# Linformer attention and maxout layer: k of two more batches turned by DMA, one turn of q issued later, two waits of loads dropped

## Chip, cores and metric

The kernel runs on one core of one Trainium2 chip. The metric is device time in microseconds (us) of one execution; lower is better. Profiles come from the hardware profiler, one execution each.

## What is computed

Eight batches of eight heads, 1024 positions of width 64, float32 in and out. k and v are first projected from 1024 positions to 64 by two shared matrices, then comes ordinary attention on the 64 projected positions, then a layer that takes the maximum of three products.

```python
k_proj = einsum('ks,bhsd->bhkd', E, k)        # 64 x 64 per head
v_proj = einsum('ks,bhsd->bhkd', F, v)
scores = matmul(q, k_proj.T) / sqrt(64)       # 1024 x 64 per head
attn   = softmax(scores)
y      = matmul(attn, v_proj)                 # 1024 x 64 per head
x      = y.transpose(0, 2, 1, 3).reshape(8192, 512)
h      = maximum(maximum(x @ w1, x @ w2), x @ w3)   # 8192 x 768
out    = h @ w_out                            # 8192 x 512
```

## The kernel before

**Stages.** The loop over batches (line 869) runs the maxout layer of batch b, and between its steps it places the attention of batch b+1. A batch has two chunks (`ch` 0 and 1) of 512 positions. A chunk is six steps of `up` (line 717; 12 matmuls each, three weight matrices by four row blocks, then a copy on ScalarE at line 733 and two maxima on VectorE at lines 737 and 678), and four steps of `down` (line 767; six matmuls each, a copy on ScalarE, and a store of 512 KB after every second one, line 792). So a chunk has steps 0 to 9, and (1, 3) in what follows is step 3 of chunk 1.

**Attention of a batch.** `load` (line 198) brings q, k and v in by three DMAs that GpSimd issues; they turn float32 into bfloat16 on the way. `qd` (line 411) lays out q in the tile `q_p` by four copies on VectorE, and then SyncE issues one DMA that transposes the whole of it, 128 x 4096, into `qT` (line 424). `kproj` (line 496) projects k: 16 matmuls and a copy to the tile `kp`, 128 x 256. Then `kp` has to be turned into `kpT`. There are two ways: `kt` (line 504) does it with two transposes on TensorE into a bank of the accumulation memory and a copy on VectorE; `kd` (line 521) does it with one DMA transpose that SyncE issues (line 524). `sc` (line 331) computes scores of a pair of heads from `qT` and `kpT` (line 221) and their exponential (line 232). `zc` (line 258) sums exponentials, inverts the sums on ScalarE, writes them to a scratch in memory (`zd`, line 278) and reads them back over all partitions with four broadcast DMAs of 512 KB (line 285). `vproj` (line 529) projects v; `vx` (line 293) multiplies the exponentials by it (line 241) and by the inverted sums (line 318), into `xT`, the input of the next batch's layer.

**Order of the work.** Each engine executes its instructions in the order in which the program writes them; the framework adds the semaphore waits for data. `plan` (line 809) is the list, written by hand, of what goes behind which step. TensorE's order is therefore `up` and `down` of batch b with the pieces of batch b+1 in between, and SyncE's queue has the stores, the scratch write and the broadcasts of `zc`, the turns of q and the turns of k, in program order. SyncE waits at the head of its queue; what comes later waits behind it. Banks of the accumulation memory are dealt out by a small model of the clock (`two`, `bank`, line 77), to whoever is free first.

For batch 2's layer, which carries the attention of batch 3 and the start of batch 4, the plan is

```python
(0, 2): [kproj(3), vproj(3), ld(4)],
(0, 3): [kt(3)],
(0, 4): [sc(3, 0, now=True), sc(3, 1)],
(0, 5): [sc(3, 2, now=True), sc(3, 3, now=True)],
(0, 7): [zc(3)],
(0, 8): [qd(4)],
(1, 3): [kproj(4), vproj(4), ld(5), vx(3, 0), vx(3, 1)],
(1, 4): [kt(4)],
(1, 7): [vx(3, 2), vx(3, 3), sc(4, 0)],
```

Batches 5, 6 and 7 already use `kd`. They are placed by the general branch at line 853 (there n = b + 1), in the layers of batches 3, 4 and 5: there kproj(n + 1), kd(n + 1) and vproj(n + 1) stand at (1, 2), and sc(n + 1, 0) four steps later, at (1, 6); the turn of q of that batch is issued at (0, 4).

**Waits added by hand.** In `load`, the DMA of q waits for the last turn of q before it (`last_T`, line 202) and, where that batch's k was turned by DMA, for that turn too (`turned`, line 204). k and v follow it in GpSimd's queue. `k_pair` (line 207) picks the layout of `kpT`: the two ways leave the pairs of heads in different places.

Of the kernel before, what the change touches and what calls it, by code (L numbers as in the profile page):

```python
# [15 lines left out]
def kernel(  # L16
# [13 lines left out]
    nc = tc.nc  # L30
# [9 lines left out]
    SI = 8  # L40
    NCT = DM // P
    NJT = DF // P
    NPAIR = H // 2
# [38 lines left out]
    def bank():  # L82
        n = min(range(8), key=lambda n: free[n])
        deal((n,))
        return psum_t[:, n, :], (n,)
# [15 lines left out]
    def copy(eng, o, i, ns=(), dt=0.65):  # L101
        done = {  # L102
            "v": nc.vector.tensor_copy, "s": nc.scalar.copy, "g": nc.gpsimd.tensor_copy
        }[eng](out=o, in_=i)
        runs(eng, clock["pe"] if ns else 0.0, dt, ns)
        return done

    def after(dma, earlier):
        tc.add_manual_dep(
            dma.ins, earlier.ins.name,  # L110
            mybir.DependencyInfo(
                mybir.DependencyClass.Sync, mybir.DependencyReason.DATA
            ),
        )


    def view(src, b):
        return src[b].rearrange("h (p si) d -> p h si d", si=SI)
# [12 lines left out]
    qkv, qTs, kpTs, vps, pTs, zis, xTs = {}, {}, {}, {}, {}, {}, {}  # L131
    last_T = {}
# [4 lines left out]
    def load_tiles(b):  # L137
        qkv[b] = tuple(
            loads.tile([P, H, SI, D], BF16, name=nm, bufs=n)
            for nm, n in (("q_t", 2), ("k_t", 1), ("v_t", 1))  # L140
        )
        return qkv[b]
# [55 lines left out]
    def load(b, which):  # L198
        tiles = qkv[b] if b in qkv else load_tiles(b)
        for i in which:  # L200
            dma = nc.gpsimd.dma_start(out=tiles[i], in_=view((q, k, v)[i], b))  # L201
            if i == 0 and b - 1 in last_T:
                after(dma, last_T[b - 1])
            if i == 0 and b - 1 in turned:
                after(dma, turned[b - 1])

    def k_pair(b, g):
        if b in turned:
# [3 lines left out]
    turned = {}  # L212
# [80 lines left out]
    def vx(b, g):  # L293
        def f():
            scale_x(b, g, 0, SI, values(b, g, 0, SI))
        return f
# [13 lines left out]
    def values(b, g, lo, nsi):  # L310
        if b not in xTs:
            xTs[b] = att.tile([P, NCT, SI, P], BF16, name="xT")
        return pair_mm(b, g, lo, nsi, lambda rows, hp: vps[b][rows, 2 * g + hp, :])

    def scale_x(b, g, lo, nsi, av):
        t, ns, ready = av
        zi, when = zis.pop((b, g, lo))
        nc.vector.tensor_tensor(  # L318
            out=xTs[b][:, g, lo:lo + nsi, :].rearrange("a (c s) p -> a c (s p)", c=2),
            in0=t, in1=zi, op=ALU.mult,  # L320
        )
        runs("v", max(ready, when), 0.17 + nsi * 0.13, ns)
# [28 lines left out]
    def proj(b, kv, t, heads, width):  # L351

        for si in range(SI):
            for hh in range(2):
                nc.tensor.matmul(  # L355
                    out=t[hh * HALF:(hh + 1) * HALF, 0:width],
                    lhsT=efT[:, si, (kv - 1) * KP:kv * KP],
                    rhs=qkv[b][kv][:, heads[hh], si, :],
                    start=(si == 0), stop=(si == SI - 1),
                )  # L360
        pe(8 * (width * 0.00042 + 0.01))
# [46 lines left out]

    q_ps = {}

    def qd(b, gs=range(NPAIR), eng="v"):

        def f():
            lo, n = gs[0], len(gs)
            if lo == 0:
                q_ps[b] = att.tile([P, NPAIR, SI, 2, D], BF16, name="q_p", bufs=1)
                qTs[b] = att.tile([P, NPAIR * SI, P], BF16, name="qT")
            q_p = q_ps[b]
            for g in gs:
                copy(  # L420
                    eng, q_p[:, g].rearrange("p si h d -> p h si d"),
                    qkv[b][0][:, 2 * g:2 * g + 2], (), 0.43,
                )
            last_T[b] = nc.sync.dma_start_transpose(
                out=qTs[b][:, lo * SI:(lo + n) * SI, :],
                in_=q_p[:, lo:lo + n].rearrange("p g si h d -> p (g si h d)"),
            )
        return f

    class Duo:  # L430
# [65 lines left out]
    def kproj(b):  # L496
        def f():
            t, ns = bank()
            proj(b, 1, t, (LO, HI), 4 * D)
            kps[b] = att.tile([P, 2, 2 * D], BF16, name="kp")  # L500
            copy("v", kps[b].rearrange("a g x -> a (g x)"), t[:, 0:4 * D], ns, 0.43)
        return f

    def kt(b):
        def f():
            t, ns = two()
            t = t.bitcast(BF16)[:, 0]
            for gg in range(2):
                nc.tensor.transpose(
                    out=t[:, gg * P:(gg + 1) * P], in_=kps[b][:, gg, :], identity=ident  # L510
                )
            pe(0.2)

            kpTs[b] = att.tile([P, NPAIR, KP], BF16, name="kpT")
            copy(
                "v", kpTs[b].rearrange("a (y x) k -> a x y k", x=2),
                t[:, 0:2 * P].rearrange("a (x y k) -> a x y k", x=2, y=2), ns, 0.3,
            )
        return f

    def kd(b):
        def f():
            kpTs[b] = att.tile([P, 2, 2 * KP], BF16, name="kpT2")
            turned[b] = nc.sync.dma_start_transpose(
                out=kpTs[b], in_=kps[b].rearrange("a g x -> a (g x)")
            )
        return f

    def vproj(b):
        def f():  # L530
            t, ns = bank()
            proj(b, 2, t, (LO, HI), 4 * D)

            vps[b] = att.tile([P, H, D], BF16, name="vp")
            for hh, hs in enumerate((LO, HI)):
                i = t[hh * HALF:(hh + 1) * HALF, 0:4 * D].rearrange("a (h d) -> a h d", d=D)
                for to in range(2):
                    copy("sv"[hh], vps[b][to * HALF:(to + 1) * HALF, hs, :], i, ns, 0.4)
        return f
# [266 lines left out]
    def ld(b, which=(0, 1, 2)):  # L806
        return lambda: load(b, which)

    def plan(b):
        n = b + 1  # L810
        if b == 0:
            return {
                (0, 6): [
                    duo[1].sums, duo[1].values, duo[0].scale, duo[1].invert,
                ],
                (0, 7): [
                    qd(1, range(2)), duo[1].scale, qd(1, range(2, 4), "s"), store_now,
                ],
                (1, 1): [kproj(1)],
                (1, 2): [kt(1)],  # L820
                (1, 3): [sc(1, 0, now=True), sc(1, 1), vproj(1), ld(2)],
                (1, 4): [za(1, 0), sc(1, 2, now=True)],
                (1, 5): [za(1, 1), sc(1, 3)],
                (1, 7): [za(1, 2)],
                (1, 8): [za(1, 3)],
            }
        if b == 1:
            return {
                (0, 0): [qd(2)],
                (0, 3): [kproj(2), vproj(2), ld(3, (0,))],  # L830
                (0, 4): [kt(2)],
                (0, 5): [sc(2, 0, now=True), sc(2, 1, now=True), sc(2, 2)],
                (0, 6): [sc(2, 3, now=True)],
                (0, 8): [zc(2, nc.gpsimd), ld(3, (1, 2))],
                (1, 1): [qd(3)],
                (1, 3): [vx(2, 0), vx(2, 1)],
                (1, 6): [vx(2, 2), vx(2, 3)],
            }
        if b == 2:
            return {  # L840
                (0, 2): [kproj(3), vproj(3), ld(4)],
                (0, 3): [kt(3)],
                (0, 4): [sc(3, 0, now=True), sc(3, 1)],
                (0, 5): [sc(3, 2, now=True), sc(3, 3, now=True)],
                (0, 7): [zc(3)],
                (0, 8): [qd(4)],
                (1, 3): [kproj(4), vproj(4), ld(5), vx(3, 0), vx(3, 1)],
                (1, 4): [kt(4)],
                (1, 7): [vx(3, 2), vx(3, 3), sc(4, 0)],
            }  # L850
        if n == B:
            return {}
        out = {
            (0, 1): [sc(n, 1, now=True), sc(n, 2, now=True), sc(n, 3)],
            (0, 3): [zc(n)],
            (1, 2): [vx(n, 0), vx(n, 1)],
            (1, 6): [vx(n, 2), vx(n, 3)],
        }
        if n + 1 < B:
            out[0, 4] = [qd(n + 1)]  # L860
            out[1, 2] = [kproj(n + 1), kd(n + 1), vproj(n + 1)] + out[1, 2]
            out[1, 6] += [sc(n + 1, 0)]
        if n + 2 < B:
            out[1, 3] = [ld(n + 2)]
        return out

    duo = [Duo(u, SPC) for u in range(2)]

    for b in range(B):
        p = plan(b)  # L870

        def behind(ch, step):
# [61 lines left out]
```

## Time and profile before

| what | value |
|---|---|
| runs of the kernel | 399.17, 399.23, 399.59 us (median 399.23) |
| the profiled execution, its own time | 399.43 us |
| its span, first to last instruction | 397.7 us |
| TensorE busy with matmuls (PE) | 390.7 us, 98% |
| VectorE (DVE) busy | 201.9 us, 51% |
| ScalarE (ACT) busy | 152.3 us, 38% |
| GpSimd (POOL) busy | 34.5 us, 9% |
| DMA row q0 (issued by GpSimd) | 29104 packets, 30.41 MB |
| DMA row q1 (issued by SyncE) | 38064 packets, 35.46 MB |
| granted TensorE clock | 0.999 |

Of the 399.43 us, 1.7 lie before the first and after the last instruction. PE is the matmul part of TensorE, PEld its weight loads; SPq is SyncE's queue as it issues DMAs. A busy time is the sum of the records of an engine. Matmul records overlap one another (a 512-column matmul has a record of 379 ns, and the next starts 216 ns after it), so a gap on TensorE is read from the distance of two starts and not from the busy time. The chain that ended last is followed back from the last instruction to what released each step. The trace also has a record of each DMA packet, with start, duration, size and row.

### The profile page before, as it was taken

The page shows a single profiled execution, that of the slowest core. Times are in us where ns is not written, and L with a number is a line of the kernel's source. Part 1 is how long each engine was busy: PE and PEld are TensorE (multiplying, and loading weights), DVE is VectorE, ACT ScalarE, POOL GpSimd, SP SyncE. Part 2 cuts the span into 40 slices and gives each one's busy share as a digit, 9 for nine tenths or more (in the row PEclk, how much of TensorE's full clock was granted, in tenths as well). Part 3 has the DMA queues.
Part 4 walks back from the last instruction along what each step waited for, and adds up shares of the span by engine and source line. Part 5 has one row for each costly group of instructions (what it writes and reads, how often), then busy time and mean ns, then how long its engine had stood idle before and what let it go on. Part 6 is the DMA issues. An engine that isn't in the chain of part 4 may idle for free.

```text
span 397.7 us, 5745 instructions
## 1 busy us (share of the span) xinstructions
PE 390.7 (98%) x2286; PEld 176.7 (44%) x2286; DVE 201.9 (51%) x312; ACT 152.3 (38%) x239; POOL 34.5 (9%) x49
## 2 busy tenths in 40 slices
PE   7999999999999999999999999999999999999996
PEld 3544443453445445444454445444454444444443
DVE  2348756761764535645374544745266443745251
ACT  2435638527222552253323532245323533132322
POOL 7350011000400200200002000200000000000000
PEclk9999999999999999999999999999999999999999
DMA  8999999987999999999979979696970138020203
GB/s 147 206 206 207 205 248 142 244 155 159 235 181 263 147 228 206 220 176 207 215 208 147 246 174 276 91 236 115 222 208 39 69 86 237 0 105 2 105 0 107
DMA packets 67339, 66.31 MB, mean 167 GB/s; under 512 B 31504, under 2 KB 59792, under 8 KB 67312
## 3 DMA queue, kind: packets, MB, share of 16 engines
q0 software_dynamic: 29104, 30.41, 47.6%
q1 hardware_dynamic: 38064, 35.46, 34.8%
q8 instruction: 18, 0.29, 0.3%
q14 instruction: 9, 0.07, 0.1%
q10 hardware_dynamic: 144, 0.07, 0.1%
HBM read 69.73 MB, written 16.97 MB: 218 GB/s over the span
## 4 chain that ended last, share of the span: by engine, by line
PE 93%; DVE 2%; DMA 2%; ACT 1%; issue 1%; POOL 0%; DVEq 0%; ACTq 0%; POOLq 0%
PE banks L668 61%; PE banks L776 20%; PE banks L355 3%; PE banks L241 2%; DMA k_t<-in_k_dram 2%; PE banks L221 2%; DVE xT L318 1%; PE banks L266 1%; ACT zi_all L307 1%; ACT zl L301 1%; PE banks L575 1%; DVE m L737 0%; PE banks L546 0%; PE banks L601 0%; PE banks L756 0%
## 5 line engine op out<-in xcount | busy, mean ns | idle before, releaser
L668 PE MATMUL banks<-xT,w_sb 128*128 128x512 bf16 x1152 | 257.1, 379 | 0.3 <-DVE xT L318 0.3
L668 PEld LDWEIGHTS <-w_sb 128*128 128x128 bf16 x1152 | 110.2, 98 | 136.6 <-issue 8.4
L737 DVE TENSOR_TENSOR m<-banks,h1s 128x512 f32<-128x512 f32 x90 | 62.1, 690 | 134.0 <-ACT h1s L733 90.1
L733 ACT COPY h1s<-banks 128x512 f32<-128x512 f32 x90 | 52.7, 585 | 122.1 <-PE banks L668 120.6
L776 PE MATMUL banks<-wout_sb,hT 128*128 128x512 bf16 x378 | 86.6, 380 | 0.1
L678 DVE TENSOR_TENSOR hT<-banks,m 128x512 bf16<-128x512 f32 x90 | 62.3, 692 | 9.4
L776 PEld LDWEIGHTS <-hT 128*128 128x128 bf16 x378 | 35.4, 98 | 47.7 <-issue 5.7
L102 ACT COPY o_sb<-banks 128x512 f32<-128x512 f32 (+2 forms) x57 | 32.9, 578 | 57.8 <-PE banks L776 57.3
L318 DVE TENSOR_TENSOR xT<-banks,zi_all 128x1024 bf16<-128x1024 f32 x28 | 33.1, 1220 | 11.7 <-PE banks L241 6.9
L232 ACT ACTIVATE pT<-banks 128x1024 bf16<-128x1024 f32 (+1 forms) x32 | 30.2, 974 | 15.4 <-PE banks L221 15.4
L201 POOL DMA_DIRECT2D q_t<-in_q_dram x7 | 6.2, 880 | 196.8 <-DMA qT<-q_p 85.1
L355 PEld LDWEIGHTS <-efT 128*64 128x64 bf16 x224 | 11.6, 110 | 3.4 <-issue 3.4
L102 DVE CAST vp<-banks 64x256 bf16<-64x256 f32 (+1 forms) x18 | 7.1, 397 | 11.7 <-ACT vp L102 9.0
L102 ACT CAST vp<-banks 64x256 bf16<-64x256 f32 x14 | 5.1, 365 | 18.3 <-PE banks L355 18.3
L241 PE MATMUL banks<-pT,vp 64*64 64x512 bf16 (+1 forms) x128 | 10.3, 375 | 0.2 <-DVE vp L102 0.2
L221 PE MATMUL banks<-qT,kpT 64*64 64x512 bf16 (+1 forms) x128 | 9.7, 372 | 0.4 <-DVE m L737 0.4
L102 DVE COPY q_p<-q_t 128x1024 bf16<-128x1024 bf16 x26 | 9.7, 433 | 0.5 <-DMA q_t<-in_q_dram 0.5
L102 DVE COPY o_sb<-banks 128x512 f32<-128x512 f32 (+1 forms) x9 | 5.6, 640 | 5.4 <-PE banks L756 4.5
L546 PE MATMUL banks<-warm_f 128*128 128x512 f32 x8 | 6.6, 977 | 1.5 <-DVE warm_f L175 1.5
L301 ACT ACTIVATE zl<-banks 128x512 f32<-128x512 f32 (+1 forms) x8 | 6.5, 811 | 3.3 <-PE banks L241 3.1
L355 PE MATMUL banks<-k_t,efT 128*64 128x256 bf16 x112 | 7.4, 276 | 0.0
L355 PE MATMUL banks<-v_t,efT 128*64 128x256 bf16 x112 | 7.3, 273 | 0.0
(73 smaller groups left out, 125.4 us busy)
## 6 DMA issues: line engine op xcount, KB each, us to landing
out_dram<-o_sb SPq DMA_DIRECT2D x30, 512.0 KB, 4.5
zi_all<-zd SPq DMA_DIRECT2D x20, 512.0 KB, 7.8
q_t<-in_q_dram POOLq DMA_DIRECT2D x7, 1024.0 KB, 10.4
k_t<-in_k_dram POOLq DMA_DIRECT2D x7, 1024.0 KB, 17.3
v_t<-in_v_dram POOLq DMA_DIRECT2D x7, 1024.0 KB, 21.9
zi_all<-zd POOLq DMA_DIRECT2D x4, 512.0 KB, 7.4
w_sb<-in_moe_w_dram POOLq DMA_DIRECT2D x4, 384.0 KB, 10.9
k_t<-in_k_dram POOLq DMA_DIRECT2D x2, 512.0 KB, 9.2
```

The source lines that it names most:

```text
L102: done = {"v": nc.vector.tensor_copy, "s": nc.scalar.copy, "g": nc.gpsimd.tensor_copy}[eng](out=o, in_=i)
L221: nc.tensor.matmul(out=t[c * HALF:(c + 1) * HALF, hp, 0:n * P], lhsT=k_pair(b, g)[rows], rhs=qTs[b][rows, at:at + n, :], start=True, stop= ...
L232: nc.scalar.activation(out=pTs[b, g, lo], in_=t, func=AF.Exp, scale=scale)
L241: nc.tensor.matmul(out=t[hp * HALF:(hp + 1) * HALF, c, 0:nsi * HALF], lhsT=w(rows, hp), rhs=p[rows, hp, :], start=True, stop=True,)
L301: nc.scalar.activation(out=zl, in_=t, func=AF.Ln)
L318: nc.vector.tensor_tensor(out=xTs[b][:, g, lo:lo + nsi, :].rearrange("a (c s) p -> a c (s p)", c=2), in0=t, in1=zi, op=ALU.mult,)
L355: nc.tensor.matmul(out=t[hh * HALF:(hh + 1) * HALF, 0:width], lhsT=efT[:, si, (kv - 1) * KP:kv * KP], rhs=qkv[b][kv][:, heads[hh], si, :], ...
L668: nc.tensor.matmul(out=h, lhsT=w_sb[i][:, ct, jt * P:(jt + 1) * P], rhs=xTs[b][:, ct, ch * SPC:(ch + 1) * SPC, :], start=(ct == first), st ...
L678: nc.vector.tensor_tensor(out=o, in0=h, in1=other, op=ALU.max)
L733: nc.scalar.copy(out=h1s, in_=h[0][0])
L737: nc.vector.tensor_tensor(out=m12, in0=h[1][0], in1=h1s, op=ALU.max)
L776: nc.tensor.matmul(out=o_ps, lhsT=hTs[b, ch][:, jt, tt * P:(tt + 1) * P], rhs=wout_sb[:, jt, :], start=(jt == 0), stop=(jt == NJT - 1),)
```

## The change

Batches 3 and 4 use `kd` in place of `kt`, directly behind their `kproj`. `qd` gets a switch, so that its copies stay at (0, 8) and the DMA of batch 4's turn of q is issued at (1, 2) by a new `qd_turn`. In SyncE's queue this puts one instruction, the store behind step (0, 9), ahead of that turn; the broadcasts of batch 3 were ahead of it already. The hand-made wait of loads for the turn of k is taken out of `load`, for all batches; the wait for the turn of q stays.

```diff
@@ load
             if i == 0 and b - 1 in last_T:
                 after(dma, last_T[b - 1])
-            if i == 0 and b - 1 in turned:
-                after(dma, turned[b - 1])
@@ qd
+    def qd_turn(b, gs=range(NPAIR)):
+        def f():
+            lo, n = gs[0], len(gs)
+            last_T[b] = nc.sync.dma_start_transpose(
+                out=qTs[b][:, lo * SI:(lo + n) * SI, :],
+                in_=q_ps[b][:, lo:lo + n].rearrange("p g si h d -> p (g si h d)"),
+            )
+        return f
+
-    def qd(b, gs=range(NPAIR), eng="v"):
+    def qd(b, gs=range(NPAIR), eng="v", turn=True):
...
-            last_T[b] = nc.sync.dma_start_transpose(
-                out=qTs[b][:, lo * SI:(lo + n) * SI, :],
-                in_=q_p[:, lo:lo + n].rearrange("p g si h d -> p (g si h d)"),
-            )
+            if turn:
+                qd_turn(b, gs)()
@@ plan, b == 2
-                (0, 2): [kproj(3), vproj(3), ld(4)],
-                (0, 3): [kt(3)],
+                (0, 2): [kproj(3), kd(3), vproj(3), ld(4)],
                 (0, 4): [sc(3, 0, now=True), sc(3, 1)],
                 (0, 5): [sc(3, 2, now=True), sc(3, 3, now=True)],
                 (0, 7): [zc(3)],
-                (0, 8): [qd(4)],
-                (1, 3): [kproj(4), vproj(4), ld(5), vx(3, 0), vx(3, 1)],
-                (1, 4): [kt(4)],
+                (0, 8): [qd(4, turn=False)],
+                (1, 2): [qd_turn(4)],
+                (1, 3): [kproj(4), kd(4), vproj(4), ld(5), vx(3, 0), vx(3, 1)],
                 (1, 7): [vx(3, 2), vx(3, 3), sc(4, 0)],
```

## Prediction

> **What bounds the kernel now.** I read the page's busy shares first, then the shares of the chain, then the chain and the timelines of TensorE and SyncE around batch 4's start, then the answers on the turned tiles.
>
> ```profile
> PE 390.7 (98%) x2286; PEld 176.7 (44%) x2286; DVE 201.9 (51%) x312; ACT 152.3 (38%) x239; POOL 34.5 (9%) x49
> PE 93%; DVE 2%; DMA 2%; ACT 1%; issue 1%; POOL 0%; DVEq 0%; ACTq 0%; POOLq 0%
> ```
>
> TensorE sets the end. A change pays only by taking matmuls from TensorE or closing a gap in its starts, and costs only by opening one. After 75 us the start records show hardly a gap besides the two around 164 us, where the change works. The chain there (start, length, what):
>
> ```profile
> 162.10 0.28 DVE kpT L102
> 162.39 0.61 DVE m L737
> 163.09 0.70 DVE hT L678
> 163.84 1.68 PE banks L776 x7
> 166.08 0.39 PE banks L221 x4
> ```
>
> TensorE waits for VectorE's last maximum, which was held up by the copy of kpT. Then its weight loads, just ahead of the scores of batch 4:
>
> ```profile
> 165.69 0.11 PEld L221 LDWEIGHTS <-kpT 64*64 64x64 bf16 x1
> 166.05 0.11 PEld L221 LDWEIGHTS <-kpT 64*64 64x64 bf16 x3 [0.25 <-issue]
> ```
>
> kpT was there at 165.69, but qT was not: the scores started at 166.05. What SyncE did before:
>
> ```profile
> 143.14 0.49 SPq L278 DMA_DIRECT2D zd<-zic  x1
> 148.49 2.60 SPq L285 DMA_DIRECT2D zi_all<-zd  x4
> 151.20 12.83 SPq L424 DMA_TRANSPOSE qT<-q_p  x1
> 164.13 6.12 SPq L792 DMA_DIRECT2D out_dram<-o_sb  x3
> qT<-q_p SPq DMA_TRANSPOSE x1, 14.8
> ```
>
> The turn of q occupies SyncE's queue from 151.20 to 164.03, because its packets stand behind 2 MB of broadcasts, and lands at 151.20 + 14.8 = 166.0. So the scores of batch 4 already start just when their input lands. The turns of k that the kernel has (batches 5 to 7; first line ns in the queue, second us to landing):
>
> ```profile
> L524 SPq DMA_TRANSPOSE kpT<-kp x3: 1181/1185/2200, 202.3 to 293.5; - x3
> DMA to landing us min/median/max: 3.0/4.1/5.0
> ```
>
> **What the Trainium skill says.** "DMA: Bandwidth & Descriptors", section "Queues, rings and completion order": on each DMA engine the descriptors of one row are consumed in ring order, and an engine goes round robin between rows by packets. The trace agrees: batch 4's turn of q has no bulk of packets before the broadcasts' last one (159.3), and batch 3's turn, beside loads of the other row, ran at 152 packets/us against 1132 alone. Hence k's turn, issued behind q's in the same row, can't overtake it. "TensorE: Matmul & The Clock Gate", section "Part 4: PE-mode transpose", gives about 275 ns for a transpose in a kernel and a copy after it; here the record is 219 ns, the distance to the next start 56 ns, the copy 0.28 us. I use the trace's.
>
> **The change, part by part.**
>
> *TensorE loses two transposes in batch 3 and two in batch 4.* Starts in batch 4: transposes at 159.82, next matmul at 159.93; batch 3: 131.89 and 132.00. So 0.11 us each, all on the path: −0.22.
>
> *VectorE loses two copies of 0.28.* Batch 3's, at 132.70, is followed by a maximum after 1.02 idle: nothing. Batch 4's is on the chain shown. Without it hT lands at 163.51 and TensorE can go on at 163.56; it gets there, 0.11 earlier than now, at 163.49 (five starts 216 ns apart, the fifth at 163.38, less 0.11). The gap of 163.38 to 163.84, 0.24 over the usual distance, shrinks to 0.07. So this point comes 163.84 − 163.56 = 0.28 earlier, the batch's own transposes included; with batch 3's 0.11, if VectorE's start follows, 0.39. TensorE would be ready for the scores at 165.70 + 0.22 − 0.39 = 165.53 in place of 166.05: **0.52 us is all that the removals can give**, and only if qT and kpT are there.
>
> *k's turn of batch 3 on SyncE.* kp is ready at 128.95 (cast 128.53 + 0.42), and SyncE has been free since 126.4. Landing: at least 3.0 after issue, so 132.0. Its packets (records: 256 of 256 B) stand behind two stores, whose last packets run at 129.5. The existing turns landed 2.1 to 2.6 after the packets ahead of them: 202.29 + 5.0 = 207.3 against 205.1; 247.10 + 4.1 = 251.2 against 248.6; 293.50 + 3.0 = 296.5 against 294.4. That gives 132.1 at most alone. Batch 4's loads start at 128.79, their packets from 130: at 152 per us the 256 take 1.7 us instead of 0.2, hence 133.6. The scores of batch 3 need it at 134.68 − 0.11 = 134.57. I take nothing: the matmuls of steps (0, 3) and (0, 4) hide it by 1.0. Its cost is between nothing and, if the tail of the landing is stretched too (135.5, an estimate), 1.0. The loads of batch 4 are held back by under 1.7 us; the scratch's landing, for which the broadcasts wait, may move by as much, because the loads end at 150 and the broadcasts' packets start as they end.
>
> *One store ahead of q's turn.* Batch 2's store of step (0, 9), now at 164.13, is issued at 151.1. It is 128 packets of 4 KB; their records after 165.5 run for 1.15 us. Placed between broadcasts and turn it puts the turn's packets back by that, or by nothing if the turn's descriptors were what was late.
>
> *q's turn.* Its bulk of 4096 packets ended 6.25 us after the last broadcast (159.3 to 165.55) in batch 4; in batches 5 to 7 it was 4.75, 4.15 and 4.3 (198.1 to 202.85, 242.1 to 246.25, 287.6 to 291.9). Batch 4's has two near-empty stretches, at 160 and 162. With the broadcasts ending at 159.2 the new end is 159.2 + 1.15 + (4.15 to 6.25) = 164.5 to 166.6. I take 165.6: the middle, and where it is now.
>
> *k's turn of batch 4.* kp is ready at 156.3, but SyncE is in q's turn until 1.5 us before that turn's end (164.03 against 165.55), 164.1. It is issued then: 164.1 + 3.0 = 167.1 at least; by packets ahead plus 2.1 to 2.6, with 165.6, 167.7 to 168.2. With both ends of q's turn: 166.6 to 169.2. I take 167.8. Until now kpT was ready at 162.38 and the turn of q was late; now the turn of k behind it is next late, by more. Behind the waiting scores on TensorE are batch 2's last two `down` steps and batch 3's layer, so nothing covers it. Scores start 0.05 after landing (166.0 to 166.05 today), at 167.85: **+1.8 us**, net of all removals, because they end in this wait. The ends are +0.6 and +3.2.
>
> *Waits of loads.* Batch 4's and 5's loads keep the wait for q's turn. Batch 5's moves with it, within 1 us; its k landed at 184.7 and is used at 199.2: nothing. Batches 6 and 7 lose the wait for k's turn and start up to 3 us earlier (208.22, 251.74 now). Their k's turn would then share with the load: 207.3 + 1.5 = 208.8 at worst, needed at 211.35. Nothing; without that cover it would cost 1.5 each.
>
> *Banks.* `kt` no longer takes two banks, so the dealing rotates for what follows. No view prices that: −0.3 to +0.3, taken at 0, since steady batches show no gap to win.
>
> Sum: profiled execution 399.43 + 1.8 = 401.2. That execution is 0.2 above the median of the runs (399.23), so I predict **401.0**.
>
> **Rivals.**
>
> *Everything lands in time.* With the store hidden in the stretches in which q's turn starved, q's bulk may end at 164.0 or before, and k's tail be shorter, 1.5. For: those empty stretches, and batches 5 to 7 with 4.2. Against: the tail was never under 2.1. It decides where k lands before 165.5; then −0.5 us, 398.7, not slower. Between this and the forecast lies a landing up to 166.8.
>
> *k of batch 3 is late as well.* Loads of batch 4 start at the same moment. If it lands at 135.5, TensorE waits 1.0 at (0, 4), and with +1.8 the time is 402.0; with the late end of k's turn of batch 4, 403.4. For: the packets of batch 3's q, seven times slower beside loads. Against: 256 packets only.
>
> *The change does only its dealing.* If k's turn of batch 4 were issued ahead of q's, or banks decided, the time would be 399.2 ± 0.3. SyncE's program order speaks against it.
>
> **How the numbers follow.** Forecast 0.70 (400.0 to 402.5). In time or nearly 0.16 (398.7 to 400.0). k of batch 3 late 0.10 (401.5 to 403.4). Dealing alone or something unseen 0.04 (398.4 to 400). A measurement here can tell about 0.2%, 0.8 us: under 398.4 is faster, over 400.0 slower. No part can give 0.8, so faster gets 0.03, from the unseen; same 0.17; slower 0.80. The range is 399.6 to 402.6: it leaves out the early third of "in time", faster, and the worst of batch 3's lateness.
>
> **What would show it.** In the new trace: SyncE's k turn directly behind q's near 164, landing near 167.8, and a gap of some 2 us in TensorE's starts ahead of L221 there, with the weight load itself waiting now. No gap at batch 3's scores near 134.5. The hT gap at 163.8 gone. Distances between batches from 170 on unchanged. Wrong if k of batch 4 lands before 166, if the gap is at batch 3's scores, or if gaps appear in later batches.

## The result, and the profile after

The changed kernel takes 401.38 us (median of 6 runs, 400.89 to 402.79) against 399.56 us for the kernel before (6 runs, 399.17 to 399.83): +1.82 us, ratio 1.0053 with a 95% interval of 1.0035 to 1.0072. (Ratios here are taken over all runs, so they are not the quotients of the medians.) I had predicted 401.0. The sum came out; the terms did not, as the profile shows at once. The profiled execution is the one of 402.79 us, the longest of the six, so its waits are larger than the median's.

The page of the changed kernel, busy times and shares of the chain (the lines shown of before were 98% and PE 93%, DMA 2%):

```profile
PE 386.8 (96%) x2240; PEld 176.1 (44%) x2282; DVE 201.5 (50%) x310; ACT 152.2 (38%) x239; POOL 34.4 (9%) x49
PE 91%; DMA 5%; ACT 1%; issue 1%; DVE 1%; POOL 0%; SPq 0%; DVEq 0%; ACTq 0%; POOLq 0%
```

There are four weight loads fewer (2286 to 2282: the four transposes) and two VectorE instructions fewer (312 to 310: the copies). The matmul records are 42 short of the weight loads, so some are missing from the trace and PE's 386.8 is not to be compared; DMA's share of the chain, from 2 to 5%, is. The chain between 126 and 172 us names both places (start, length, what):

```profile
128.45 0.43 DVE kp L102
128.89 0.02 issue
128.90 8.51 DMA kpT<-kp
137.42 0.04 issue
137.46 0.63 PE banks L219 x8
...
167.18 2.31 DMA kpT<-kp
169.48 0.04 issue
169.53 0.41 PE banks L219 x4
```

The turn of k of batch 3, issued at 128.90, took 8.51 us to land, and TensorE waited for it at batch 3's scores. The turn of k of batch 4 took 2.31 us and ended the second wait. SyncE's queue at these points:

```profile
128.90 1.18 SPq L529 DMA_TRANSPOSE kpT<-kp  x1
...
151.00 2.61 SPq L283 DMA_DIRECT2D zi_all<-zd  x4
153.71 0.64 SPq L797 DMA_DIRECT2D out_dram<-o_sb  x1
154.46 12.63 SPq L412 DMA_TRANSPOSE qT<-q_p  x1
167.18 1.20 SPq L529 DMA_TRANSPOSE kpT<-kp  x1
```

The order is the one that the prediction used: broadcasts, one store, q's turn for 12.63 us, and k's turn directly behind it. In the kernel before, batch 3's scores had started at 134.68 without a wait for kpT; an idle time of 0.42 ahead of these weight loads is usual:

```profile
134.68 0.14 PEld L221 LDWEIGHTS <-kpT 64*64 64x64 bf16 x8 [0.42 <-DVE m L737]
```

Starts of the same instructions in the two profiles tell where time is lost:

| first instruction of | before | after | later by |
|---|---|---|---|
| scores of batch 3 | 134.68 | 137.46 | 2.78 |
| projection of k of batch 4 | 154.79 | 157.57 | 2.78 |
| vx(3, 2), just ahead of batch 4's scores | 165.45 | 168.03 | 2.58 |
| scores of batch 4 | 166.05 | 169.53 | 3.48 |
| next scores of batch 4 | 174.27 | 177.74 | 3.47 |
| last instruction (span) | 397.7 | 401.0 | 3.3 |

2.78 of it arises at batch 3's scores, where the prediction had put nothing. 0.20 comes back between the next two rows, where the removed transposes and the copy ahead of hT were. 0.90 arises at batch 4's scores. After that the two traces run in step.

### The profile page after: what moved, and what is told of

The parts are those of the page before. It is cut to its first block, busy times and chain, and to the rows that moved or that the text cites. A ratio compares the mean times of both kernels' runs of the same rounds, so it can differ in the third digit from the quotient of the medians.

```text
span 401.0 us, 5698 instructions
## 1 busy us (share of the span) xinstructions
PE 386.8 (96%) x2240; PEld 176.1 (44%) x2282; DVE 201.5 (50%) x310; ACT 152.2 (38%) x239; POOL 34.4 (9%) x49
## 4 chain that ended last, share of the span: by engine, by line
PE 91%; DMA 5%; ACT 1%; issue 1%; DVE 1%; POOL 0%; SPq 0%; DVEq 0%; ACTq 0%; POOLq 0%
PE banks L673 60%; PE banks L781 20%; PE banks L353 3%; DMA kpT<-kp 3%; PE banks L239 2%; DMA k_t<-in_k_dram 2%; PE banks L219 2%; PE banks L264 1%; DVE xT L316 1%; ACT zi_all L305 1%; ACT zl L299 1%; PE banks L580 1%; PE banks L551 0%; PE banks L606 0%; PE banks L761 0%
## 5 line engine op out<-in xcount | busy, mean ns | idle before, releaser
L673 PE MATMUL banks<-xT,w_sb 128*128 128x512 bf16 x1119 | 254.1, 379 | 2.4 <-issue 0.6
L781 PE MATMUL banks<-wout_sb,hT 128*128 128x512 bf16 x370 | 85.5, 379 | 0.9 <-issue 0.6
L219 PEld LDWEIGHTS <-kpT 64*64 64x64 bf16 x128 | 2.9, 105 | 10.0 <-DMA kpT<-kp 4.7
```

The lines of the kernel that those rows point to most:

```text
L219: nc.tensor.matmul(out=t[c * HALF:(c + 1) * HALF, hp, 0:n * P], lhsT=k_pair(b, g)[rows], rhs=qTs[b][rows, at:at + n, :], start=True, stop= ...
L673: nc.tensor.matmul(out=h, lhsT=w_sb[i][:, ct, jt * P:(jt + 1) * P], rhs=xTs[b][:, ct, ch * SPC:(ch + 1) * SPC, :], start=(ct == first), st ...
L781: nc.tensor.matmul(out=o_ps, lhsT=hTs[b, ch][:, jt, tt * P:(tt + 1) * P], rhs=wout_sb[:, jt, :], start=(jt == 0), stop=(jt == NJT - 1),)
```

## The experiments

Three theories. A: batch 3's k is late because batch 4's loads start beside it, and batch 4's because store, turn of q and turn of k all have to pass SyncE's row ahead of the scores. B: the turn of batch 3's k is slow behind the two stores ahead of it in its row, and the loads do not matter. C, my prediction: only batch 4 counts. All times are against runs of the kernel before that were taken beside them on the same chip. Loads don't wait for k's turn in any of these kernels, as in the changed one, except where a run says so.

### Batch 3 alone

```diff
@@ from the changed kernel, plan, b == 2
-                (0, 8): [qd(4, turn=False)],
-                (1, 2): [qd_turn(4)],
-                (1, 3): [kproj(4), kd(4), vproj(4), ld(5), vx(3, 0), vx(3, 1)],
+                (0, 8): [qd(4)],
+                (1, 3): [kproj(4), vproj(4), ld(5), vx(3, 0), vx(3, 1)],
+                (1, 4): [kt(4)],
```

> Only batch 3's k is turned by DMA; batch 4 keeps TensorE's transposes and its old turn of q; the loads don't wait for k's turn. Theory A (batch 4's loads, which start at the same moment, stretch k's turn of batch 3): it lands 5 us or more after its issue, TensorE waits 1 to 3 us at batch 3's scores, the time is 1 to 2.8 us over before. Theory B (the turn of k is slow behind the two stores in its own row, whatever the loads do): the same here. Theory C (my prediction: only batch 4's turn counts, and batch 3's wait in the profile was one execution's accident): no wait at batch 3's scores, -0.1 us.

Measured: 400.60 against 399.41 us, +1.19; ratio 1.0042 (1.0014 to 1.0070). The runs spread from 399.22 to 404.67. In the profiled execution the turn took 6.4 us from issue to landing, and the weight load at batch 3's scores waited:

```profile
kpT<-kp SPq DMA_TRANSPOSE x1, 6.4
135.46 0.14 PEld L219 LDWEIGHTS <-kpT 64*64 64x64 bf16 x8 [1.27 <-DMA kpT<-kp]
```

1.27 idle where 0.42 is usual: 0.85 lost in this execution. Theory C falls: batch 3's lateness is no accident of one execution, but its size varies, from about nothing to several microseconds. Not all of the spread is landing: the two longest runs, 403.01 and 404.67 us, also have the lowest mean clocks of the nine, 0.995 and 0.996 against 0.998 to 1.000.

### Batch 4 alone

```diff
@@ from the changed kernel, plan, b == 2
-                (0, 2): [kproj(3), kd(3), vproj(3), ld(4)],
+                (0, 2): [kproj(3), vproj(3), ld(4)],
+                (0, 3): [kt(3)],
```

> Batch 3 keeps TensorE's transposes; batch 4's k is turned by DMA behind the late turn of q. Theories A and B: TensorE waits about 1 us at batch 4's scores, 0.5 to 1.2 us over before. Theory C: the whole +1.8 us is here.

Measured: 400.58 us, +1.17; ratio 1.0024 (1.0012 to 1.0035), and hardly any spread (400.33 to 400.78). As A expected. SyncE's queue:

```profile
151.62 0.67 SPq L797 DMA_DIRECT2D out_dram<-o_sb  x1
152.40 12.40 SPq L412 DMA_TRANSPOSE qT<-q_p  x1
164.90 1.20 SPq L529 DMA_TRANSPOSE kpT<-kp  x1
```

q's turn landed at 152.40 + 14.4 = 166.8 and k's at 164.90 + 2.3 = 167.2. So k's turn ended only 0.4 after q's, and scores started at 167.24. The two single runs add up to 2.36; the whole change costs 1.82. The spread of batch 3's part is larger than that difference, so I draw nothing from it.

### The load waits for k's turn again

```diff
@@ from the changed kernel, load
             if i == 0 and b - 1 in last_T:
                 after(dma, last_T[b - 1])
+            if i == 0 and b - 1 in turned:
+                after(dma, turned[b - 1])
```

> The changed kernel with the removed lines put back: the load of q waits for k's turn too. Theory A: k's turn of batch 3 lands about 3 us after its issue and the wait at batch 3's scores is gone; batch 4's loads start some 4 us later and end as much later, the broadcasts of batch 3 with them, so that the turns of batch 4 may come 1 to 4 us later than in before: +1 to +4 us in all, the wait now at batch 4's scores. Theory B: the wait at batch 3's scores stays. Theory C: no wait at batch 3's scores here nor without the lines; +1.8 us in both.

Measured: 402.88 us, +3.47; ratio 1.0080 (1.0066 to 1.0094). GpSimd's queue issued batch 4's loads at 131.76 in place of 128.05, and k's turn, in the same place of SyncE's queue behind the same stores, now took 2.3 us:

```profile
125.28 1.00 SPq L799 DMA_DIRECT2D out_dram<-o_sb  x2
128.88 1.17 SPq L531 DMA_TRANSPOSE kpT<-kp  x1
kpT<-kp SPq DMA_TRANSPOSE x1, 2.3
```

It landed at 131.2, 3 us ahead of the scores, and there was no wait there. Everything else being as in the changed kernel, 8.5 became 2.3 us when the loads stood back. That speaks for A and against B. But the cost moved and grew. q's turn of batch 4 landed at 168.0 (152.80 + 15.2; 166.8 in the run of batch 4 alone), k's at 168.4, and the weight load at batch 4's scores waited:

```profile
168.44 0.11 PEld L221 LDWEIGHTS <-kpT 64*64 64x64 bf16 x4 [2.98 <-DMA kpT<-kp]
...
169.14 0.15 PEld L783 LDWEIGHTS <-hT 128*128 128x128 bf16 x1 [0.25 <-issue]
169.57 0.15 PEld L783 LDWEIGHTS <-hT 128*128 128x128 bf16 x1 [0.28 <-issue]
```

Behind the wait the weight loads take 0.15 in place of 0.10 us and follow one another in 0.43 in place of 0.22. The stretches before, in and after it show why; the columns are the stretch, its length, busy time of PE, PEld, DVE, ACT and POOL, the granted clock, the DMA share and GB/s:

```profile
160.00:168.40 8.40, 5.69 (x31) 2.12 (x29) 5.79 (x7) 1.75 (x3) 0.00 (x0) 1.00 1.07 225
168.40:173.00 4.60, 4.34 (x15) 1.73 (x17) 0.00 (x0) 1.48 (x2) 2.63 (x3) 0.63 0.77 167
173.00:178.00 5.00, 5.00 (x25) 2.25 (x23) 1.73 (x3) 1.79 (x4) 0.00 (x0) 1.00 1.13 158
```

For 4.6 us the clock was 0.63: at that rate 4.6 x 0.37 = 1.7 us are lost, on top of a wait of 2.5. Three of the six runs show this loss in their mean clock (0.994 to 0.995, 402.90 to 403.50 us), three don't (0.999 to 1.000, 401.88 to 402.87 us). So leaving this hand-made wait out was not the fault; with it the median is worse by 1.65, and the median of the three runs without the loss, 401.92, is still 2.5 over the kernel before.

### k's turn in the middle of the loads

```diff
@@ from the changed kernel
+    def k_behind_q_load():
+        after(turned[3], q_loads[4])
...
-                (0, 2): [kproj(3), kd(3), vproj(3), ld(4)],
+                (0, 2): [kproj(3), vproj(3), ld(4), kd(3), k_behind_q_load],
```

> The changed kernel with k's turn of batch 3 made to wait until batch 4's q has landed, so that it runs in the middle of the loads of k and v and not at their start. TensorE waits for it at batch 3's scores in any case, some 8 us; what counts is the time from its issue to its landing. If any load beside it stretches it: 5 us or more, as in the profiles with the load starting beside it (6.4 and 8.5). If only a load's start does it: 2.3 to 3.5 us.

Measured: 411.6 us, nearly all of it the 10 us for which TensorE waits by construction and the slow clock behind that. `q_loads` holds the DMA of q that `load` issues. What counts is SyncE's issue and the time to landing:

```profile
137.33 1.18 SPq L535 DMA_TRANSPOSE kpT<-kp  x1
kpT<-kp SPq DMA_TRANSPOSE x1, 6.7
```

6.7 us in the steady middle of the loads of k and v, with no store ahead in its row. So it is not only the start of a load that stretches a turn. Packet records show two shapes of it. Where the load's packets were already running, the turn's came late: in the changed kernel's profile the load's ran from 129.6 and k's 256 packets from 133.5 to 136.9, the first 4.6 us after SyncE's issue; here the first came at 141.2, 3.9 us after it. In the run of batch 3 alone k's packets came first, through by 130.9, and the load's from 130.65; there the 4-byte packets of SyncE's row, which I take to report completion, came only at 134.0 to 135.2. With the loads held back they came at 130.5 to 130.9. Why a few hundred packets wait that long is not settled by these runs.

### The store alone

```diff
@@ from the kernel before, with qd and qd_turn of the changed one, plan, b == 2
-                (0, 8): [qd(4)],
+                (0, 8): [qd(4, turn=False)],
+                (1, 2): [qd_turn(4)],
```

> The kernel before with one thing changed: batch 4's turn of q is issued at (1, 2), so behind one store. By the prediction's term the turn lands 0 to 1.15 us later, which the scores of batch 4 feel in full: 0 to +1.1 us. If the turn's own descriptors are what is late, 0.

The loads' wait for k's turn stands here as in the kernel before. Measured: 400.24 against 399.41 us, +0.83; ratio 1.0022 (1.0014 to 1.0030, 22 runs). q landed at 152.81 + 14.2 = 167.0 and the scores started at 167.05, 0.87 after the weight load ahead of them (0.36 in the kernel before). The term of the prediction, 0 to 1.15 and fully felt, holds.

### Batch 4's k ahead of its q

```diff
@@ from the run of batch 4 alone, plan, b == 2
-                (1, 2): [qd_turn(4)],
-                (1, 3): [kproj(4), kd(4), vproj(4), ld(5), vx(3, 0), vx(3, 1)],
+                (1, 3): [kproj(4), kd(4), qd_turn(4), vproj(4), ld(5), vx(3, 0), vx(3, 1)],
```

> Batch 3's k by TensorE; batch 4's k turned by DMA ahead of its turn of q in SyncE's queue, and the store of step (0, 9) ahead of both. If the order of k behind q costs, k lands long before batch 4's scores and they wait for q alone; q lands as in the run with only the store moved. Theory A: between +0.5 and +0.9 us over before, some 0.4 under the run with k behind q (+1.17). If k's place doesn't matter: +1.2 us again.

Measured: 400.31 against 399.45 us, +0.86; ratio 1.0021 (1.0012 to 1.0030). As with the store alone, and TensorE's wait now is for qT. k's place behind q is worth the difference to +1.17, some 0.3 us, but across these two runs that is within the noise. Against the run of the store alone, taken beside that of batch 4 alone, it is 0.34 (95% interval, resampled from the runs: 0.04 to 0.57), barely clear of it.

### Batch 4's turn of q where it was

```diff
@@ from the run of batch 4 alone, plan, b == 2
-                (0, 8): [qd(4, turn=False)],
-                (1, 2): [qd_turn(4)],
+                (0, 8): [qd(4)],
```

> Batch 3's k by TensorE, batch 4's turn of q where it was in before (ahead of the store), batch 4's k turned by DMA behind it. Theory A (the store is most of batch 4's cost, k's turn ends 0.4 us after q's): k lands near 166.4, +0.3 to +0.5 us. The prediction's working (k lands 2.1 to 2.6 us after q's last packet): near 167.7, +1.7 us.

Measured: 400.70 us, +1.25; ratio 1.0037 (1.0022 to 1.0052). My expectation missed, because I forgot where the store then stands:

```profile
151.18 12.45 SPq L412 DMA_TRANSPOSE qT<-q_p  x1
163.73 0.53 SPq L797 DMA_DIRECT2D out_dram<-o_sb  x1
164.36 1.39 SPq L529 DMA_TRANSPOSE kpT<-kp  x1
```

q lands early again, at 151.18 + 14.4 = 165.6, but the store now lies between the two turns, and k lands at 164.36 + 2.9 = 167.3. So between the two turns the store costs what it costs ahead of both (+1.17), within the noise: in both places store, q and k all have to pass before the scores. Moving q's turn behind the store, as the change does, cost nothing that shows beside this alternative. The store behind q and k in that order was not tried.

### The store behind both turns

```diff
@@ from the run with k ahead of q
-            if (b, ch, tt) == (0, 0, 1):
+            if (b, ch, tt) in ((0, 0, 1), (2, 0, 3)):
                 stores.append(store)
...
-                (1, 3): [kproj(4), kd(4), qd_turn(4), vproj(4), ld(5), vx(3, 0), vx(3, 1)],
+                (1, 3): [kproj(4), kd(4), qd_turn(4), store_now, vproj(4), ld(5), vx(3, 0), vx(3, 1)],
```

> As the run with k ahead of q for batch 4 (+0.85), but the store of step (0, 9) is issued behind both turns. If the store is what remained of batch 4's cost, q lands about 1 us earlier, near 165.3 to 166.0, and the time is -0.5 to 0 us against before. If it is q's turn itself that is late once it waits for batch 4's kp (issued near 157 and not at 151): +0.5 us or more, as with the store ahead.

A store in `stores` is kept back until `store_now` issues it.

Measured: 399.26 against 399.34 us; ratio 1.0001 (0.9993 to 1.0009). Batch 4's cost is gone. SyncE's queue shows the price of it:

```profile
148.79 2.60 SPq L283 DMA_DIRECT2D zi_all<-zd  x4
156.37 1.20 SPq L529 DMA_TRANSPOSE kpT<-kp  x1
157.66 5.96 SPq L412 DMA_TRANSPOSE qT<-q_p  x1
163.71 6.18 SPq L797 DMA_DIRECT2D out_dram<-o_sb  x3
```

q's turn is issued 6 us later than in the kernel before (157.66 against 151.20) and lands no later: 157.66 + 8.0 = 165.7. It had only been waiting in SyncE's queue behind the broadcasts' packets; 5.96 us of issue replace 12.83.

### Batch 3's k one step earlier

```diff
@@ from the run of batch 3 alone, plan, b == 2
-                (0, 2): [kproj(3), kd(3), vproj(3), ld(4)],
+                (0, 1): [kproj(3), kd(3)],
+                (0, 2): [vproj(3), ld(4)],
```

> Only batch 3's k by DMA, as in the first run of this kind (+1.2), but its projection and turn one step earlier, at (0, 1): issued near 126.4, 2 us ahead of the loads. Theory A (loads beside it stretch it): it lands before 131, no wait at batch 3's scores, -0.3 to +0.2 us. Theory B (it is slow behind the two stores of its row): issued while both are in the row, it still lands 5 us or more after issue; its scores may hide that, so the time from issue to landing decides.

Measured: 399.30 against 399.34 us; ratio 0.9996 (0.9987 to 1.0004), 398.75 to 399.73 in 13 runs. Both the cost and the spread of batch 3's turn are gone. Issued at 126.52, behind both stores, it landed 4.3 us later, at 130.8:

```profile
kpT<-kp SPq DMA_TRANSPOSE x1, 4.3
```

Most of that was ahead of the load, whose packets ran from 129.6. Theory B's 5 us or more didn't come.

### The waits of loads alone

```diff
@@ from the kernel before, load
-            if i == 0 and b - 1 in turned:
-                after(dma, turned[b - 1])
```

> The kernel before without the loads' wait for k's turn, which batches 6 and 7 have; nothing else changed. Prediction's term and theory A: k's turns of batches 5 and 6 are four steps ahead of their scores, so 0 (within 0.3 us). Rival: the earlier loads stretch those turns as they do batch 3's, and the scores of batch 5 or 6 wait: +1 us or more.

Measured: 399.35 against 399.45 us; ratio 0.9994 (0.9985 to 1.0003). No time is lost, as predicted, but the turn of batch 6 was stretched all the same. The three turns of k here, which were 3.0, 4.1 and 5.0 us in the kernel before:

```profile
DMA to landing us min/median/max: 3.7/5.1/8.0
```

The 8.0 is batch 6's. In the kernel before this turn took 4.1 us and the next load waited for it; here the load starts at 246.32, 0.7 us ahead of the turn. The turn lands at 255.0 and is used at 257.3, so the distance hides it. Batch 6 is a control that every run has: in the ten profiles of kernels without the wait its turn took 6.6 to 8.3 us, in the three with it (before, the store alone, the load waiting again) 4.0 to 4.4. Without the wait the load's packets start 0.9 to 1.5 us after the turn's issue, and the turn's own end 5.7 to 7.8 us after it, against 3.1 to 3.8 with the wait. Batch 7's, with no load beside it, took 2.8 to 3.7 in all thirteen. So theory A's reading of the load doesn't rest on batch 3 alone.

### Both remedies

```diff
@@ from the run with the store behind both turns, plan, b == 2
-                (0, 2): [kproj(3), vproj(3), ld(4)],
-                (0, 3): [kt(3)],
+                (0, 1): [kproj(3), kd(3)],
+                (0, 2): [vproj(3), ld(4)],
```

> Both remedies: batch 3's k one step earlier, batch 4's k and q turns ahead of the store. If both causes are right nothing waits for a turn of k: -0.6 to 0 us against before, the best of all. If the wait at either batch's scores stays: +0.5 us or more.

Measured: 399.10 against 399.34 us; ratio 0.9993 (0.9984 to 1.0002). No wait for a turn of k is left. It has the lowest median of all the kernels, but the interval includes 1: a kernel faster than before is not shown, and the removals' bound of 0.5 us says why not much can be.

## Why the prediction was right, and where it wasn't

**What bounds.** That TensorE sets the end, that the removals can give no more than 0.52 us, and that the change must pay in waits for turned tiles, held. With every such wait taken away the gain was 0.24 us, within the measurement of nothing.

**k's turn of batch 3: the step that failed.** I took nothing: a landing at 133.6, 4.6 us after issue, hidden by 1.0 us, with a cost of at most 1.0. It costs about 1.2 on the median of its own run, 0.85 and 2.78 in two profiles. I had reckoned the load as a lower packet rate only (1.5 us more) and named the stretched tail as a mere bound. Landing took 6.4, 8.5 and 6.7 us beside loads, and 2.3 without. The term for the waits of batches 6 and 7 has the same fault: it allowed 1.5 us of stretch, and batch 6's turn took 3.9 more; only its distance saved it. The trace of before had a sign of such a delay. Batch 3's turn of q was issued at 105.35 with nothing ahead of it in its row, and its first packet came at 110.98, just as the last of the broadcasts in GpSimd's row ended (111.01). I took this turn's rate beside the loads and not its late start. The Trainium skill's page "DMA: Bandwidth & Descriptors", section "Issuing engines are not separate DMA queues", says that DMAs from all queues run on the same engines and interleave. Once begun, k's packets did run among the load's (133.5 to 136.9 in the changed kernel's profile); of the late start and the late completion the section says nothing.

**k's turn of batch 4: the wait right, its terms mis-sized.** I had +1.8 there, all of it on k's place: q's last packet was to stay at 165.6, store included, and k to land 2.1 to 2.6 us after it. By itself batch 4's part costs 1.17. In that profile q's last packet came near 166.3, so 0.7 later, and k landed at 167.2, 0.9 after it and 0.4 after q. The 2.1 to 2.6 came from turns behind stores. Of the 1.17 the store is 0.83 and k's place the rest, 0.34, with the interval given above. (The 159.3 that I took for the last packet of the broadcasts is the end of their bulk; 22 of the 512 end later, up to 160.15.)

**Two errors of opposite sign** thus made the predicted sum meet the median: batch 4 0.6 too much, batch 3 about 1.2 too little, with the two parts overlapping by an amount that the spread doesn't let me fix. That the number came out is luck. By a sign that the prediction itself set, that it is wrong if the gap is at batch 3's scores, its account is wrong. My chance of 0.10 for "k of batch 3 late as well" was much too small, and its time of 402.0 to 403.4 fits only the longer runs.

**The rest.** The store: 0 to 1.15 predicted, 0.83. The waits of batches 6 and 7: no time predicted, none measured. Banks: nothing seen after 170. The gap ahead of hT: predicted to shrink from 0.24 to 0.07 over the usual 0.22; in the profile after it is 0.37 wide, so 0.15 is left, and up to there the removals gave 0.20 us where I had 0.39.

## What to carry to other kernels

A small DMA saves engine time only if its landing is priced beside what else will be in flight: for such a turn that was 2.3 to 5.2 us with no more than stores or another turn ahead of it in its row, 6.4 to 8.5 us beside a running load, and no packet rate told it. Give it a step more of distance, or issue it ahead of the load, rather than make the load wait: the load's delay came back, larger, in the chain behind it. In a queue that runs in order, count everything that has to land before the consumer, and move what nobody waits for (here a store) to the end.

## What was not expected of the hardware

After the wait of 2.5 us in the profile with the load waiting, TensorE's granted clock was 0.63 over the next 4.6 us: 0.50 from 168.9 to 172.3, full before and behind. After the 2.9 us wait in the changed kernel's profile it stayed at full rate:

```profile
134.00:137.40 3.40, 0.57 (x3) 0.07 (x1) 1.20 (x2) 0.00 (x0) 0.00 (x0) 1.00 1.30 181
137.40:142.00 4.60, 4.49 (x31) 1.76 (x33) 1.87 (x4) 3.36 (x4) 0.00 (x0) 1.00 1.24 209
```

In the run with k's turn in the middle of the loads, TensorE waited 9.6 us; the clock fell to 0.50 some 2 us into the wait and stayed there until 6 us after it. The Trainium skill's page "TensorE: Matmul & The Clock Gate", section "Why this matters for your kernels", warns of idle gaps over about 3 us; here a shorter gap lowered the clock and a longer one did not, so the length alone does not decide. Runs of one and the same kernel differ too, as the mean clocks of the six runs with the load waiting show.
